# Fused attention, gated experts and a spatial gating MLP on one core: six warm-up products, batch 1's first adds on VectorE, the last batch's factors in three buffers with W2 behind them, w_out's last row off GpSimd

## The chip, the cores and the metric

The kernel runs on one core of one Trainium2 chip. The metric is the device time of one execution in microseconds (us). TensorE is called PE in the profile, VectorE DVE, ScalarE ACT, GpSimd POOL, SyncE SP. SyncE only issues transfers (DMA).

## The reference

Three layers follow one another on 4 batches of 448 positions. All of it is float32.

```python
scores = cap * np.tanh(scale * q @ k.T / cap)            # 12 heads of 64
x = softmax(scores) @ v                                  # then x: 4 x 448 x 768
# experts: 4 small causal attentions of width 64, two chosen for each position
ye = softmax(causal((x @ wq[e]) @ (x @ wk[e]).T / 8)) @ (x @ wv[e]) @ wo[e]
x = sum of the two chosen w[e] * ye
h = gelu(x @ w_in)                                       # 768 -> 1024
u, v = halves of h
gated = u * (w_sg @ layernorm(v) + b_sg)                 # w_sg mixes positions
out = x + gated @ w_out                                  # 512 -> 768
```

## The kernel before

Matmuls of the first layer run in float32; later ones split each operand into a rounded part and a remainder (names ending in h and l) and add three products. Since the experts' output enters the MLP through wo and w_in alone, the kernel multiplies these two first into W2 (tiles `parts`, `wt`, then `w2_d` in DRAM, read back as `w2_h` and `w2_l`).

**Attention** goes in slots, one for each pair of heads, six pairs for each of four batches (`slot`, L319). In a slot TensorE makes scores `s`, ScalarE applies Tanh and Exp into `p`, TensorE multiplies with the values into `po` and adds up the softmax sums from `pb`, a running sum of the `p` tiles. `scores` (L224) makes the first add of `pb` (L242): on VectorE in batch 0, on GpSimd in the others. `add_up` (L250) makes the other two on VectorE. At the very start, before anything has been loaded, `WARM` products of zeros keep TensorE busy (L771).

**Slots carry side work** at places named a, w, p and n. Through the first ten slots that is the conversion of w_in and its products into W2 (`prepare_weights`); then the experts of the batch before (`PLAN`), and the conversion of w_out, a row or half a row at a time (`w_out`, L423: VectorE unpacks two 32-bit halves, GpSimd rounds, subtracts and adds, SyncE stores both parts in DRAM as `wud`).

**Normalising** a batch: the sums go to DRAM (`rd`), come back spread over partitions as `ri` (`spread`), VectorE takes the reciprocal (`inverted`), they go to DRAM again, and come back copied over 64 partitions as factors `rb` (`load_rb`, L370, two transfers each). `over_sums` multiplies an output block `os` by its `rb`; `in_parts` splits it into `xh` and `xl`. A batch has three blocks. The factors' tiles are two (`rb0`, `rb1`), so the third block's loads take the first one's tile. `normed` (L389) says at which places of which slots this is done; for the last batch `slot` does it after the last pair (L349 to L355) and `experts_end` (L640) loads the third factors.

**The end** runs the experts of batches 2 and 3 and the MLP side by side (`experts_end`, `mlp_a`, `mlp_b`, `mlp_c`, ORD 3). `mlp_weights(0)` reads W2 through GpSimd's queue at high priority (L821 to L824); `mlp_weights(2)` converts w_out's last row in three pieces (L817). Temporary tiles `tmp` of the MLP and w_out's pieces share six buffers. In this part the order on each engine is chosen by the scheduler from the program and its own clock; before it, the engines keep the program's order, except SyncE, whose order is always the scheduler's.

Each engine works through its instructions in order; SyncE's queue likewise holds a transfer back until what it waits for is there, and all behind it.

Of the kernel before, what the change touches and what calls it, by code (L numbers as in the profile page):

```python
# [33 lines left out]
LO64, HI64 = (float(np.array([w], np.uint32).view(np.float32)[0]) for w in (0x38000000, 0x47F00000))  # L34
LAG, RATIO, LRATIO, AHEAD, EQ, ORD, L1, EL, WC, NCST, D0, D1, D2, PB, XE, SE, START, WARM, Q2, CK, PE, CP_, AD, WR, KD, PTA, PTE, XHA, LGA, SL, GL, YL, GA, GB = 0.4, .9, .35, 150, 1, 3, 1, 1, 500, 1, 3, 3, 2, 1, 1, 0, 500, 12, 1, 2, 0, 0, 0, 6, 0, 3, 2, 4, 4, 0, 0, 0, 1, 0
GC = float(np.float32(np.sqrt(2.0 / np.pi)))
# [38 lines left out]
def build(ctx: ExitStack, tc: tile.TileContext, a: dict):  # L75
    nc = tc.nc
# [147 lines left out]
    def scores(b, hp, h, qp, kp, then=None):  # L224
# [15 lines left out]
        if h == 0:  # L240
            pb = at.tile([128, 2, S], F32, tag="pb", name=f"pb{b}_{hp}", bufs=3)
            (dve if b == 0 else pool_e).tensor_tensor(pb, p[:, :, 0, :], p[:, :, 1, :], op=ALU.add)  # L242
            pend[b, hp] = (p, pb)
        else:
            p0, pb = pend[b, hp]
            pend[b, hp] = (p0, p, pb)
            if n == 2:
                ptail[b, hp // 2] = p[:, :, 1, :]
# [70 lines left out]
    def slot(i, side):  # L319
# [29 lines left out]
        if i == len(pairs):  # L349
            drain(sums(B - 1, HP // 2 - 1))  # L350
            invert(B - 1)
            spread(B - 1)
            inverted(B - 1)
            load_rb(B - 1, 0)
            load_rb(B - 1, 1)  # L355
        side("p")
# [12 lines left out]

    def load_rb(b, h2):  # L370
        rb = rbs[b, h2] = xp.tile([128, 2, S], F32, tag=f"rb{h2 % 2}", name=f"rb{b}_{h2}")
        for r in range(2):
            nc.sync.dma_start(rb[64 * r:64 * r + 64],
                              rb_d[b][r::2, h2:h2 + 1, :].rearrange("r o s -> o r s").to_broadcast([64, 2, S]))
# [14 lines left out]
    def normed(n, place):  # L389
# [14 lines left out]
        elif step == (3, "w"):  # L404
            over_sums(b, 0)
            over_sums(b, 1)
            load_rb(b, 2)
        elif b == 0 and step == (3, "a1"):
            in_parts(b, 0)
            in_parts(b, 1)  # L410
        elif step == (4, "w"):
            if b:
                in_parts(b, 0)
            over_sums(b, 2)
            if not b:
                in_parts(b, 2)
        elif b and step == (4, "a1"):
            in_parts(b, 1)
            in_parts(b, 2)

    projected = []

    def w_out(k, i, of, w, me):  # L423

# [6 lines left out]
        p, e = from64(w, me[:, :n], me[:, n:])  # L431
        rnd("p", hi, p)
        pool_e.tensor_tensor(p, p, hi.bitcast(F32), op=ALU.subtract)
        pool_e.tensor_tensor(lo, p, e, op=ALU.add)
        for t in range(2):
# [204 lines left out]
    def experts_end():  # L640
# [3 lines left out]
        def steps():  # L644
# [12 lines left out]
            over_sums(l, 1)  # L657
            load_rb(l, 2)
            yield from weigh(b, 1, 0, 1)
# [153 lines left out]
    def mlp_weights(part):  # L813
# [3 lines left out]
        if part == 2:  # L817
            for i in range(3):
                yield from w_out(3, i, 3, *[lambda dt, name: ml.tile([128, 512], dt, tag="tmp", name=name, bufs=6)] * 2)
            return  # L820
        for k in range(2):  # L821
            with tc.high_priority(12000):
                nc.gpsimd.dma_start(w2_h[:, k, :], w2_d[0][:, k, :])
                nc.gpsimd.dma_start(w2_l[:, k, :], w2_d[1][:, k, :])  # L824
        nc.sync.dma_start(gln, a["g_ln"])
# [140 lines left out]
    g_places = [(mg, "gh", "gl"), (mo, "pe2", "pe3"), (mo, "pt0", "pt1"), (mg, "gh", "gl")]  # L966
    MLP = 8 * 1278.0 + 8 * 1120.0 + 4 * 1120.0 + 36 * 560.0 + 17.0
    drain(mlp_weights(0))
    C = 36 * 560.0
# [77 lines left out]
```

## Time and profile before

| | us |
|---|---|
| runs, median (lowest to highest of 3) | 548.62 (545.62 to 549.73) |
| profiled execution | 545.04 |
| its span, first to last instruction | 543.2 |
| TensorE busy | 516.1 |
| VectorE busy | 333.2 |
| ScalarE busy | 319.0 |
| GpSimd busy | 132.2 |

The profile is of one execution. A timeline row gives start, length, engine, line, operation, what is written and read, and in brackets how long the engine had been idle before it and what ended that. The line is mostly that of a helper (L106 for three engines, L121 for matmuls), so tiles identify a row. A row "x4" joins four instructions that follow one another.

### The profile page before, as it was taken

How to read it: one execution, taken by the hardware profiler on the slowest of the kernel's cores; microseconds unless marked ns; L12 is line 12 of the kernel's file. 1: busy time of each engine (PE TensorE's matmuls, PEld its weight loads, DVE VectorE, ACT ScalarE, POOL GpSimd, SP SyncE). 2: the span in 40 equal slices, each digit the busy share in tenths (PEclk: the TensorE clock that was granted, in tenths of full speed). 3: DMA queues.
4: the chain of work that ended last, by engine and by line, in shares of the span. 5: the costliest groups of instructions: out<-in, count | busy, mean ns of one | idle time of the engine just before them, and what ended most of it. 6: DMA issues, size and time to landing. Idle time of an engine off the chain costs nothing.

```text
span 543.2 us, 7596 instructions
## 1 busy us (share of the span) xinstructions
PE 516.1 (95%) x2732; PEld 336.6 (62%) x2732; DVE 333.2 (61%) x683; ACT 319.0 (59%) x529; POOL 132.2 (24%) x151
## 2 busy tenths in 40 slices
PE   7999999899999999999998698999899999999997
PEld 2233333455655555554476457768678889889996
DVE  3899999874466646456724596755722796484300
ACT  5989888688777766777631573542544364252211
POOL 0000232251451341441540829004502010010000
PEclk9999999999999999999999899799999999999999
DMA  8955527643514224240129011110611000001011
GB/s 306 344 168 159 188 70 201 203 154 113 153 60 142 74 87 120 71 107 1 59 73 293 18 39 49 42 46 0 219 67 52 1 1 35 34 36 50 36 51 68
DMA packets 34693, 54.16 MB, mean 100 GB/s; under 512 B 5536, under 2 KB 29536, under 8 KB 34656
## 3 DMA queue, kind: packets, MB, share of 16 engines
q1 hardware_dynamic: 33360, 48.22, 28.6%
q0 software_dynamic: 1152, 5.24, 2.8%
q8 instruction: 21, 0.34, 0.3%
q10 hardware_dynamic: 144, 0.23, 0.1%
q14 instruction: 16, 0.13, 0.1%
HBM read 41.92 MB, written 11.75 MB: 99 GB/s over the span
## 4 chain that ended last, share of the span: by engine, by line
PE 71%; DVE 9%; ACT 5%; DMA 5%; POOL 4%; issue 4%; SPq 1%; DVEq 0%; POOLq 0%; ACTq 0%
PE o L121 15%; PE s L121 9%; PE po L121 9%; PE sp L121 7%; PE qk L121 5%; PE v L121 4%; PE hv L121 4%; PE hu L121 4%; PE w2ps L121 3%; PE a L121 3%; ACT p L106 3%; PE av L121 3%; DMA rb<-rd 3%; PE tr L542 2%; POOL pe L106 2%
## 5 line engine op out<-in xcount | busy, mean ns | idle before, releaser
L106 ACT ACTIVATE p<-s,tsc 128x896 f32<-128x896 f32 x84 | 80.7, 1005 | 26.0 <-PE s L121 20.2
L121 PE MATMUL s<-qp,kp 64*128 64x448 f32 (+1 forms) x384 | 77.8, 566 | 3.6 <-ACT p L106 3.6
L106 POOL TENSOR_TENSOR pb<-p 128x896 f32<-128x896 f32 x18 | 41.0, 2280 | 160.4 <-ACT p L106 153.6
L106 ACT ACTIVATE p<-p,capt 128x1792 f32<-128x1792 f32 (+1 forms) x48 | 77.0, 1604 | 1.1
L106 DVE TENSOR_TENSOR pb<-pb,p 128x896 f32<-128x896 f32 (+1 forms) x48 | 56.8, 1183 | 20.3 <-ACT p L106 11.1
L121 PE MATMUL po<-p,vv 128*64 128x448 f32 x288 | 59.4, 548 | 0.0
L121 PEld LDWEIGHTS s<-qp,kp 64*128 64x128 f32 (+1 forms) x384 | 27.0, 173 | 48.6 <-issue 23.4
L106 POOL TENSOR_SCALAR pe<-pe,cs 112x112 f32<-112x112 f32 (+1 forms) x64 | 39.7, 642 | 56.0 <-DVE cs L106 56.0
L106 ACT ACTIVATE pe<-a,m 112x112 f32<-112x112 f32 (+3 forms) x64 | 31.4, 495 | 26.7 <-DVE m L106 23.6
L106 DVE CUSTOM_DVE_ANT_0 a<-a,neg 112x112 f32<-112x112 f32 (+3 forms) x64 | 28.2, 463 | 29.8 <-PE a L121 29.3
L121 PEld LDWEIGHTS po<-p,vv 128*64 128x64 f32 x288 | 18.5, 136 | 37.9 <-issue 35.1
L121 PE MATMUL qk<-xh,wqk_h 128*128 128x448 f32 x96 | 37.3, 390 | 4.1 <-DVE xh L106 2.3
L106 POOL TENSOR_TENSOR rstd<-rstd,mhalf 112x1 f32<-112x1 f32 x16 | 10.2, 637 | 104.8 <-DVE rstd L106 104.8
L121 PE MATMUL o<-gh,wu_h 128*128 128x448 f32 x96 | 35.3, 368 | 0.0
L542 PE MATMUL tr<-ident,pe 112*112 112x112 f32 x160 | 25.3, 265 | 10.5 <-POOL pe L106 4.6
L106 ACT ACTIVATE ob<-o 128x448 f32<-128x448 f32 x24 | 13.0, 542 | 37.8 <-PE o L121 37.7
L121 PE MATMUL o<-gl,wu_h 128*128 128x448 f32 x96 | 35.2, 366 | 0.0
L121 PE MATMUL qk<-xh,wqk_l 128*128 128x448 f32 x96 | 35.1, 366 | 0.0
L121 PE MATMUL o<-gh,wu_l 128*128 128x448 f32 x96 | 34.8, 367 | 0.0
L106 ACT ACTIVATE pt<-tr 112x112 f32<-112x112 f32 (+3 forms) x48 | 18.8, 403 | 22.7 <-PE tr L542 22.3
L542 PEld LDWEIGHTS tr<-ident,pe 112*112 112x112 f32 x160 | 17.8, 134 | 18.6 <-issue 8.1
L121 PE MATMUL a<-qk 64*112 64x112 f32 (+3 forms) x128 | 28.6, 440 | 0.8 <-ACT qk L106 0.6
(227 smaller groups left out, 1113.2 us busy)
## 6 DMA issues: line engine op xcount, KB each, us to landing
rb<-rd SPq DMA_DIRECT2D x24, 224.0 KB, 5.4
out_dram<-ob SPq DMA_DIRECT2D x24, 224.0 KB, 1.9
kp<-in_kT_dram SPq DMA_DIRECT2D x23, 224.0 KB, 3.5
qp<-in_qT_dram SPq DMA_DIRECT2D x23, 224.0 KB, 3.7
vv<-in_v_dram SPq DMA_DIRECT2D x24, 192.0 KB, 3.3
wuw<-in_w_out_dram SPq DMA_DIRECT2D x6, 384.0 KB, 3.4
wud<-wuw SPq DMA_DIRECT2D x12, 192.0 KB, 1.9
ws<-in_wqk_dram SPq DMA_DIRECT2D x4, 384.0 KB, 5.7
```

Source lines behind the costliest of these rows:

```text
L106: ins = f(*args, **kw)
L121: pin(nc.tensor.matmul(*args, **kw))
L542: pin(nc.tensor.transpose(g[:CP, j * CP:(j + 1) * CP], pe[:, j * CP:(j + 1) * CP], ident))
```

## The change

Six edits in the text:

- `WARM` goes from 12 to 6.
- In `scores`, batch 1's pairs 0 to 3 make their first add of `pb` on VectorE.
- In `normed`, batch 0's third block is multiplied and split in slot 3's place p, not slot 4's place w.
- For the last batch, `spread`, `inverted` and the loads of factors move behind the attention, ahead of `mlp_weights(0)`, and the third factors get a tile of their own (in `ypool`, tag y), loaded with the other two.
- W2 is read through SyncE's queue, with no priority.
- `w_out` gets an argument `by`; for the last row ScalarE rounds, and VectorE subtracts and adds.

```diff
--- before.py
+++ after.py
@@ -32,7 +32,7 @@
 BIG = float(np.finfo(np.float32).max)
 
 LO64, HI64 = (float(np.array([w], np.uint32).view(np.float32)[0]) for w in (0x38000000, 0x47F00000))
-LAG, RATIO, LRATIO, AHEAD, EQ, ORD, L1, EL, WC, NCST, D0, D1, D2, PB, XE, SE, START, WARM, Q2, CK, PE, CP_, AD, WR, KD, PTA, PTE, XHA, LGA, SL, GL, YL, GA, GB = 0.4, .9, .35, 150, 1, 3, 1, 1, 500, 1, 3, 3, 2, 1, 1, 0, 500, 12, 1, 2, 0, 0, 0, 6, 0, 3, 2, 4, 4, 0, 0, 0, 1, 0
+LAG, RATIO, LRATIO, AHEAD, EQ, ORD, L1, EL, WC, NCST, D0, D1, D2, PB, XE, SE, START, WARM, Q2, CK, PE, CP_, AD, WR, KD, PTA, PTE, XHA, LGA, SL, GL, YL, GA, GB = 0.4, .9, .35, 150, 1, 3, 1, 1, 500, 1, 3, 3, 2, 1, 1, 0, 500, 6, 1, 2, 0, 0, 0, 6, 0, 3, 2, 4, 4, 0, 0, 0, 1, 0
 GC = float(np.float32(np.sqrt(2.0 / np.pi)))
 GQ = float(np.float32(np.sqrt(0.044715)))
 
@@ -239,7 +239,7 @@
         act.activation(p[:, :, :n, :], p[:, :, :n, :], AF.Exp, scale=capt)
         if h == 0:
             pb = at.tile([128, 2, S], F32, tag="pb", name=f"pb{b}_{hp}", bufs=3)
-            (dve if b == 0 else pool_e).tensor_tensor(pb, p[:, :, 0, :], p[:, :, 1, :], op=ALU.add)
+            (dve if b == 0 or (b, hp) < (1, 4) else pool_e).tensor_tensor(pb, p[:, :, 0, :], p[:, :, 1, :], op=ALU.add)
             pend[b, hp] = (p, pb)
         else:
             p0, pb = pend[b, hp]
@@ -349,10 +349,6 @@
         if i == len(pairs):
             drain(sums(B - 1, HP // 2 - 1))
             invert(B - 1)
-            spread(B - 1)
-            inverted(B - 1)
-            load_rb(B - 1, 0)
-            load_rb(B - 1, 1)
         side("p")
         if 0 < i < len(pairs):
             b, hp = pairs[i - 1]
@@ -367,8 +363,8 @@
 
     rbs = {}
 
-    def load_rb(b, h2):
-        rb = rbs[b, h2] = xp.tile([128, 2, S], F32, tag=f"rb{h2 % 2}", name=f"rb{b}_{h2}")
+    def load_rb(b, h2, pool=xp, tag=None):
+        rb = rbs[b, h2] = pool.tile([128, 2, S], F32, tag=tag or f"rb{h2 % 2}", name=f"rb{b}_{h2}")
         for r in range(2):
             nc.sync.dma_start(rb[64 * r:64 * r + 64],
                               rb_d[b][r::2, h2:h2 + 1, :].rearrange("r o s -> o r s").to_broadcast([64, 2, S]))
@@ -408,19 +404,19 @@
         elif b == 0 and step == (3, "a1"):
             in_parts(b, 0)
             in_parts(b, 1)
-        elif step == (4, "w"):
-            if b:
-                in_parts(b, 0)
+        elif b == 0 and step == (3, "p"):
             over_sums(b, 2)
-            if not b:
-                in_parts(b, 2)
+            in_parts(b, 2)
+        elif b and step == (4, "w"):
+            in_parts(b, 0)
+            over_sums(b, 2)
         elif b and step == (4, "a1"):
             in_parts(b, 1)
             in_parts(b, 2)
 
     projected = []
 
-    def w_out(k, i, of, w, me):
+    def w_out(k, i, of, w, me, by=None):
 
         n = DM // of
         o = slice(i * n, (i + 1) * n)
@@ -429,9 +425,10 @@
         nc.sync.dma_start(w.bitcast(I64), a["w_out"][:, k, o])
         yield WC
         p, e = from64(w, me[:, :n], me[:, n:])
-        rnd("p", hi, p)
-        pool_e.tensor_tensor(p, p, hi.bitcast(F32), op=ALU.subtract)
-        pool_e.tensor_tensor(lo, p, e, op=ALU.add)
+        rnd(by or "p", hi, p)
+        diff = dve if by else pool_e
+        diff.tensor_tensor(p, p, hi.bitcast(F32), op=ALU.subtract)
+        diff.tensor_tensor(lo, p, e, op=ALU.add)
         for t in range(2):
             nc.sync.dma_start(wu_d[t][:, k, o], (hi, lo)[t].bitcast(F32))
         yield 1.0
@@ -655,7 +652,6 @@
             yield from turn(b, 0, 0)
             over_sums(l, 0)
             over_sums(l, 1)
-            load_rb(l, 2)
             yield from weigh(b, 1, 0, 1)
             yield from turn(b, 0, 1)
             in_parts(l, 0)
@@ -816,12 +812,11 @@
             return
         if part == 2:
             for i in range(3):
-                yield from w_out(3, i, 3, *[lambda dt, name: ml.tile([128, 512], dt, tag="tmp", name=name, bufs=6)] * 2)
+                yield from w_out(3, i, 3, *[lambda dt, name: ml.tile([128, 512], dt, tag="tmp", name=name, bufs=6)] * 2, by="a")
             return
         for k in range(2):
-            with tc.high_priority(12000):
-                nc.gpsimd.dma_start(w2_h[:, k, :], w2_d[0][:, k, :])
-                nc.gpsimd.dma_start(w2_l[:, k, :], w2_d[1][:, k, :])
+            nc.sync.dma_start(w2_h[:, k, :].bitcast(F32), w2_d[0][:, k, :])
+            nc.sync.dma_start(w2_l[:, k, :].bitcast(F32), w2_d[1][:, k, :])
         nc.sync.dma_start(gln, a["g_ln"])
         nc.sync.dma_start(bsg, a["b_sg"].to_broadcast([128, S]))
         dve.memset(mhalf, -0.5)
@@ -965,6 +960,11 @@
     v_places = [(ml, "vh", "vl"), (xp, "xh", "xl")] * 2
     g_places = [(mg, "gh", "gl"), (mo, "pe2", "pe3"), (mo, "pt0", "pt1"), (mg, "gh", "gl")]
     MLP = 8 * 1278.0 + 8 * 1120.0 + 4 * 1120.0 + 36 * 560.0 + 17.0
+    spread(B - 1)
+    inverted(B - 1)
+    load_rb(B - 1, 0)
+    load_rb(B - 1, 1)
+    load_rb(B - 1, 2, ypool, "y")
     drain(mlp_weights(0))
     C = 36 * 560.0
     if ORD == 2:
```

SyncE's queue, from the last batch's sums on. `rs`, `rd`, `ri` and `rb` are the sums, their DRAM tile, their spread form and the factors; `wuw` is a half row of w_out and `wud` its store; the digit behind a name is batch or row. Before:

```order
L299 DMA rd3_2396<-rs3_2039 128x448
L308 DMA ri3_2398<-rd3_2396 32x42 x4
L314 DMA rd3_2396<-ri3_2398 32x42 x4
L373 DMA rb3_0_2408<-rd3_2396 64x2x448 x2
L373 DMA rb3_1_2411<-rd3_2396 64x2x448 x2
L436 DMA wud0_79<-wuw2_1_2333 128x384
L373 DMA rb3_2_2841<-rd3_2396 64x2x448 x2
L436 DMA wud1_80<-wuw2_1_2333 128x384
L830 DMA w_sgT0_2522<-in_w_sgT_dram 112x448
```

And in the change:

```order
L308 DMA ri3_2392<-rd3_2390 32x42 x4
L433 DMA wud0_79<-wuw2_1_2327 128x384
L314 DMA rd3_2390<-ri3_2392 32x42 x2
L433 DMA wud1_80<-wuw2_1_2327 128x384
L314 DMA rd3_2390<-ri3_2392 32x42 x2
L818 DMA w2_h_2488<-w2d0_81 128x1024
L369 DMA rb3_0_2503<-rd3_2390 64x2x448 x2
L369 DMA rb3_1_2506<-rd3_2390 64x2x448 x2
L369 DMA rb3_2_2509<-rd3_2390 64x2x448 x2
L819 DMA w2_l_2489<-w2d1_82 128x1024
L818 DMA w2_h_2488<-w2d0_81 128x1024
```

Two stores of w_out and the first quarter of W2 (`w2_h`) now stand ahead of the six factor transfers, which follow one another; the other three quarters stand behind them.

VectorE, at the products of the last batch's blocks (`os3`) with their factors; `a2_0_*_3` are expert scores of 448 columns of batch 2 that the instruction masks. Before:

```order
L106 RECIPROCAL ri3_2398<-ri3_2398 128x42
L106 TENSOR_SCALAR wum2_1_2334<-wuw2_1_2333 128x384
...
L106 SCALAR_TENSOR_TENSOR wum2_1_2334<-wuw2_1_2333,wum2_1_2334 128x384
L106 TENSOR_TENSOR os3_1_1971<-os3_1_1971,rb3_0_2408 128x896
L106 ISA a2_0_0_3_2625,m2_0_0_3_2629<-a2_0_0_3_2625,neg_74 112x448
...
L106 TENSOR_TENSOR os3_3_2180<-os3_3_2180,rb3_1_2411 128x896
L106 ISA a2_0_1_3_2626,m2_0_1_3_2633<-a2_0_1_3_2626,neg_74 112x448
...
L106 TENSOR_TENSOR os3_5_2369<-os3_5_2369,rb3_2_2841 128x896
...
L106 TENSOR_TENSOR gt2_2657<-vp2_2414 112x64
```

And in the change:

```order
L106 TENSOR_SCALAR wum2_1_2328<-wuw2_1_2327 128x384
...
L106 SCALAR_TENSOR_TENSOR wum2_1_2328<-wuw2_1_2327,wum2_1_2328 128x384
L106 RECIPROCAL ri3_2392<-ri3_2392 128x42
L106 ISA a2_0_0_2_2535,m2_0_0_2_2539<-a2_0_0_2_2535,neg_74 112x336
...
L106 ISA a2_0_0_3_2622,m2_0_0_3_2626<-a2_0_0_3_2622,neg_74 112x448
...
L106 ISA a2_0_1_3_2623,m2_0_1_3_2630<-a2_0_1_3_2623,neg_74 112x448
...
L106 TENSOR_TENSOR os3_1_1965<-os3_1_1965,rb3_0_2503 128x896
...
L106 TENSOR_TENSOR os3_3_2174<-os3_3_2174,rb3_1_2506 128x896
...
L106 TENSOR_TENSOR os3_5_2363<-os3_5_2363,rb3_2_2509 128x896
...
L106 TENSOR_TENSOR gt2_2654<-vp2_2393 112x64
```

w_out's unpacking now ends ahead of the reciprocal (`ri3`, which before stood ahead of it), and the two masks of 448 columns stand ahead of all three products.

TensorE, behind these expert scores (`v2_3` is a chunk of the experts' values, `hv0` and `hu0` are the MLP's first products with W2). Before:

```order
L121 MATMUL a2_0_0_3_2625<-qk2_0_2219 112x448
L121 MATMUL a2_0_1_3_2626<-qk2_0_2219 112x448
L121 MATMUL v2_3_2637<-wvg_h_77,xh2_2170 112x260
L121 MATMUL v2_3_2637<-wvg_l_78,xh2_2170 112x260
L121 MATMUL v2_3_2637<-wvg_h_77,xl2_2171 112x260
```

And in the change:

```order
L121 MATMUL a2_0_0_3_2622<-qk2_0_2213 112x448
L121 MATMUL a2_0_1_3_2623<-qk2_0_2213 112x448
L121 MATMUL hv0_0_2553<-w2_h_2488,yh0_2547 112x512
L121 MATMUL hv0_1_2614<-w2_h_2488,yh0_2547 112x512
L121 MATMUL hv0_2_2709<-w2_h_2488,yh0_2547 112x512
L121 MATMUL hv0_3_2750<-w2_h_2488,yh0_2547 112x512
L121 MATMUL hu0_0_2927<-yh0_2547,w2_h_2488 128x448
L121 MATMUL hu0_0_2927<-yl0_2548,w2_h_2488 128x448
L121 MATMUL v2_3_2634<-wvg_h_77,xh2_2164 112x260
L121 MATMUL v2_3_2634<-wvg_l_78,xh2_2164 112x260
```

Six products with W2 now stand ahead of the chunk of values. From about 373 us of the profile on, TensorE's order is that of before.

## Rows read from the trace of the kernel before

**Rows 1.** The page, part 1: busy us, share of the span, instructions of TensorE.
```profile
PE 516.1 (95%) x2732; PEld 336.6 (62%) x2732; DVE 333.2 (61%) x683; ACT 319.0 (59%) x529; POOL 132.2 (24%) x151
```

**Rows 2.** Busy time by stretch (us; x counts instructions), granted clock, DMA share, GB/s.
```profile
84.00:104.00 20.00, 17.58 (x80) 6.60 (x80) 19.70 (x20) 16.80 (x19) 5.51 (x2) 1.00 0.79 223
298.00:312.00 14.00, 9.44 (x41) 6.94 (x39) 8.52 (x22) 7.22 (x15) 10.60 (x11) 0.88 0.09 24
340.00:352.00 12.00, 11.22 (x43) 8.86 (x44) 8.71 (x22) 6.63 (x20) 0.76 (x2) 0.72 0.08 25
```

**Rows 3.** Timeline (start, us, engine line op out<-in, idle before), the start; one tile's durations; landings.
```profile
0.73 0.41 ACTq L106 DMA_DIRECT2D qp<-in_qT_dram  x1
1.32 5.30 PE L121 MATMUL warm<-z 128*128 128x512 bf16 x12 [1.32 <-POOL z L106]
6.54 2.01 PE L121 MATMUL s<-qp,kp 64*128 64x448 f32 x8
7.85 1.01 ACT L106 ACTIVATE p<-s,tsc 128x896 f32<-128x896 f32 x1 [5.18 <-PE s L121]
L121 PE MATMUL s<-qp,kp x72: 536/536/876, 6.5 to 38.6; 64*128 64x448 f32 x56, 64*64 64x448 f32 x16
qp<-in_qT_dram ACTq DMA_DIRECT2D x1, 224.0 KB, 3.0
```

**Rows 4.** Timeline of VectorE, GpSimd and TensorE, 78 to 105 us.
```profile
87.08 2.20 DVE L106 TENSOR_TENSOR pb<-pb,p 128x896 f32<-128x896 f32 x2
92.08 2.50 DVE L106 CAST xh<-os 128x896 fp32r<-128x896 f32 x1
95.63 0.62 DVE L106 CAST xh<-os 128x896 fp32r<-128x896 f32 x1
91.42 2.69 POOL L106 TENSOR_TENSOR pb<-p 128x896 f32<-128x896 f32 x1 [9.63 <-ACT p L106]
104.32 0.48 PE L121 MATMUL qk<-xh,wqk_h 128*128 128x448 f32 x1 [2.29 <-DVE xh L106]
```

**Rows 5.** Timeline of SyncE's queue, VectorE and TensorE, 279 to 305 us; median landings (DMA issues).
```profile
279.63 3.69 SPq L373 DMA_DIRECT2D rb<-rd  x4
286.41 1.28 SPq L373 DMA_DIRECT2D rb<-rd  x2
296.15 1.09 DVE L106 TENSOR_TENSOR os<-os,rb 128x896 f32<-128x896 f32 x1 [5.92 <-DMA rb<-rd]
282.68 1.01 PE L121 MATMUL a<-qk 64*112 64x448 f32 x4
287.79 0.47 PE L121 MATMUL qk<-xh,wqk_h 128*128 128x448 f32 x1 [1.76 <-ACT pe L106]
302.11 0.31 PE L542 MATMUL tr<-ident,pe 112*112 112x112 f32 x1 [2.93 <-POOL pe L106]
304.28 0.62 PE L542 MATMUL tr<-ident,pe 112*112 112x112 f32 x2 [1.63 <-POOL pe L106]
rb<-rd SPq DMA_DIRECT2D x24, 224.0 KB, 5.4
wi_4w<-in_w_in_dram SPq DMA_DIRECT2D x2, 512.0 KB, 3.7
w_l<-w2d POOLq DMA_DIRECT2D x2, 512.0 KB, 10.5
```

**Rows 6.** Timeline of GpSimd, ScalarE, VectorE and TensorE, 327 to 341 us; waits of SyncE's queue.
```profile
327.75 7.56 POOL L106 TENSOR_SCALAR pe<-pe,cs 112x112 f32<-112x112 f32 x8
338.19 0.54 ACT L106 ACTIVATE gsu<-hu 128x448 f32<-128x448 f32 x1 [3.50 <-POOL wuw L106]
338.77 0.62 DVE L106 SCALAR_TENSOR_TENSOR gsu<-gsu,hu 128x448 f32<-128x448 f32 x1 [4.51 <-ACT gsu L106]
340.78 0.47 PE L121 MATMUL hu<-yh,w_h 128*128 128x448 f32 x1 [2.61 <-DVE u L106]
SPq L436 <- POOL wuw L106: 63.2, 14, 21.3
```

## The prediction

> **What bounds the kernel now.** I read the busy times first. TensorE is busy 516.1 of 543.2 us [rows 1], so at most 27 us are to be had by taking its waits away, and no shorter engine matters except where TensorE waits for it. The busy times by stretch then show where it waits: 2.4 us in 84 to 104 us, where VectorE has no time left (19.70 of 20), 4.6 us in 298 to 312 us and 0.8 us in 340 to 352 us [rows 2]. In the last two the granted clock falls as well, to a mean of 0.88 and 0.72. There are two levels, 1.2 and 2.4 GHz, so a mean of c over t us stands for (1-c) x 2t at the lower level and costs (1-c) x t of full-speed work: 0.12 x 14 = 1.7 us and 0.28 x 12 = 3.4 us. Before each fall TensorE had stood idle for 2.93 [rows 5] and 2.61 us [rows 6]. Last I read the timeline around those places, to see whom TensorE waits for. The change touches all of them.
>
> **Part A, six warm-up products instead of twelve.** The twelve take 5.30 us, 0.44 each, from 1.32 us, and the first scores start at 6.54 [rows 3]. Their queries are sent for at 0.73 and land 3.0 later, at 3.7, so nothing but the products holds them. Six products end at 1.32 + 6 x 0.44 = 4.0, 2.6 earlier. Not all of it comes back. The first score matmuls take up to 876 ns, later ones 536, so up to about 7 us the lower level holds, although the stretch view prints 1.00 there (its clock record has not begun). Now the first scores lie in that time wholly. From their start to the first Tanh it is 7.85 - 6.54 = 1.31 now; at most 1.31 x 876/536 = 2.1 then, so Tanh starts at 6.1, 1.7 earlier. The second tile of scores takes 2.1 more, to 8.2, and its Tanh could have started at 7.85 + 1.01 = 8.9 before: 0.7 earlier. ScalarE's chain of Tanh and Exp sets the pace until 20 us, so I take 1.2, between the two; bounds 0 (clock later) and 2.6.
>
> By the Trainium skill, page "TensorE: Matmul & The Clock Gate", section "Part 1: The HAM clock gate (the "warmup" mystery)", activity releases the clock and the place where it rises is not tied to the kernel's start but varies from run to run. One profile cannot show the spread; it is a reason for the rival on the clock below.
>
> **Part B, batch 1's first adds of head pairs 0 to 3 on VectorE.** Four adds leave GpSimd (2.69 us for the one at 91.42) and cost VectorE what an add of the same size costs it, 2.20 / 2 = 1.10 each [rows 4], 4.4 together. But a GpSimd add is not free for VectorE: the cast that starts under the one at 91.42 takes 2.50 where the same cast alone takes 0.62, 1.88 more. The other three stretch a VectorE instruction in the same way. At 1.88 each VectorE gains 4 x (1.88 - 1.10) = 3.1 us before 104 us. What TensorE can take of that is its wait for the cast of the third normalised block, 2.29 at 104.32. The change also puts that block's product, cast and remainder ahead of the slot's running sum, but its factors' two loads behind four more transfers on SyncE's queue, and ScalarE waits for that sum, so some comes back as a wait of ScalarE. I take 1.8; bounds 0 (loads late) and 2.7 (the wait and some smaller ones).
>
> **Part C, last batch's factors in three buffers, W2 behind them.** Before, the third pair of factor loads waited until the first product had freed its buffer: the first four issue from 279.63, the third pair at 286.41, in the midst of W2's transfers, and VectorE stands 5.92 us at the third product until 296.15 [rows 5]. Behind it in VectorE's order stand the gates and the softmax factors, behind these GpSimd's scaling, and behind that the transposes for which TensorE waits 2.93 and 1.63. A wait of 1.76 at 287.79 comes from the same queue: the masks of 448 columns stood between the products; now they stand ahead of all three. Together 6.3 us of idle TensorE, and 1.7 us of lower clock.
>
> What is late next? On SyncE's queue two stores of w_out and W2's first quarter now stand ahead of the factors. The stores wait for GpSimd, whose input VectorE now prepares in its idle time before the reciprocal, so I cost them at their issue; with these and W2's quarter the factors start at about 281 instead of 279.63. Six issues at 3.69 / 4 = 0.92 end at 286.5, and with the median landing of 5.4 the last is there at 291 to 292, 4 to 5 us earlier than 296.15. From the third product to the transpose it took 302.11 - 296.15 = 6.0, now 297 to 298. TensorE came there at 302.11 - 2.93 = 299.2; less the 1.76, plus some 0.6 of W2 products moved ahead and 1.0 of a new wait, it comes at 299.0. So that wait goes, with 1.5 to spare.
>
> The new wait: six products with W2's first quarter now stand right behind the matmuls of 448 columns, which end at 282.68 + 1.01 = 283.7. The quarter (512 KB) is issued at about 280.2; a load of that size on this queue lands in 3.7 us, one of the same size from GpSimd's queue in 10.5. I take 4.5, near the first, because it is on the same queue and only two stores and small transfers stand ahead of it: 1.0 us of wait. Sum of C: 6.3 + 1.7 - 1.0 = 7.0; bounds -0.7 (landing 10.5 makes the wait 7.0, and the clock falls there instead: 6.3 - 7.0) and 8.0.
>
> **Part D, w_out's last row off GpSimd.** At 340.78 TensorE has waited 2.61 us: the up-projection's buffers are free only when GpSimd has done the row's pieces, and GpSimd starts on them after 7.56 us of scaling that begins at 327.75. ScalarE (3.50) and VectorE (4.51 until 338.77) stand idle for it [rows 6]. Now ScalarE rounds and VectorE subtracts and adds. Six operations of 256 columns cost VectorE at least 1.10 x 256/896 = 0.31 and at most what GpSimd's eight scalings take, 0.95 each: 1.9 to 5.7 us. I take 0.4 each, 2.4, near the smaller row since it is the same engine and kind; this fits in the 4.51 us in which it stood. ScalarE's three roundings fit in its 3.50. So the 2.61 goes and of the 3.4 us of lower clock I count 2.9, as other short waits are near: 5.5; bounds 1.4 (rival 3) and 6.0. W2's loads off GpSimd's queue cost nothing elsewhere, since GpSimd is idle there.
>
> By the Trainium skill, page "SBUF — State Buffer", section "Who interferes with whom", a VectorE instruction with two SBUF inputs and a GpSimd instruction that reads SBUF exclude each other, and the second to issue blocks in full. By that rule the six operations could each stand behind a scaling; the cast in rows 4 agrees that a VectorE instruction waits. This is the third rival below.
>
> **Sum.** 1.2 + 1.8 + 7.0 + 5.5 = 15.5 us. Against the profiled execution's own 545.04 us that is 529.5. The median of the runs, 548.62, lies 3.6 above it, and a timed median is asked for: 548.6 - 15.5 = 533.1.
>
> **Rivals.**
> (1) W2 is late, 0.11. If the quarter takes 10.5 us as from GpSimd's queue, it lands at 290.7: 7.0 us of wait instead of 1.0, and the clock falls there instead, 1.7. For it: TensorE is in order, and the loads of this stretch are the slowest of the kernel. Against it: the quarter is now first, not mixed with the factors. 533.1 + 6.0 + 1.7 = 540.8.
> (2) The clock rises later at the start, 0.06. If the lower level lasts 5.8 us longer (as long again as it did now), that costs up to 2.9 of full-speed work: part A turns from -1.2 to +1.7 and the time is 536.0. Against it: until 20 us ScalarE sets the pace.
> (3) VectorE is late at w_out, 0.05. At 5.7 us for the six it runs 5.7 - 4.5 = 1.2 over its idle time, TensorE still waits that long, and so the clock's 2.9 may stay lost: 533.1 + 4.1 = 537.2.
> (4) Slower than before, 0.05. SyncE's queue stands at a w_out store ahead of the factors' way back. For it: it has waited up to 21.3 us for GpSimd at such a store [rows 6], and everything on VectorE is queued behind the factors. The slack is the 1.5 us of part C. A stand of 21.3 would cost 19.8: 533.1 + 19.8 = 552.9. It decides against the change from a stand of 15.5 + 1.5 = 17.0 us on. Against it: the store's input is ready on VectorE some 2 us before the reciprocal.
> (5) Two or more parts miss their gain together, 0.11: with C and D at their lower bounds, 533.1 + 7.7 + 4.1 = 544.9.
>
> **Chances and range.** The forecast, all parts within their bounds with no rival, has 0.62. Within 1% (543.1 to 554.1) is about what a measurement of this kernel can't tell from no change. The forecast and rivals 1 to 3 lie below that: 0.84 faster. Rival 5 and part of rival 4 lie within: 0.13. Slower by over 1%: 0.03. The range reaches from 527.0 (all upper bounds at once, 19.3, give 529.3; the rest is for runs in which the clock falls less often) to 542.0, which takes in rivals 1 to 3 and leaves out 4 and 5, 0.16.
>
> **What would show it.** Warm-up ends near 4.0 and the first Tanh starts near 6. No GpSimd add before 95 us; the wait of 2.29 for the third block's cast gone. All six factor loads issued in one run from about 281; the third product starts by 292; no wait over 1 us at the transposes near 302 and the granted clock of that stretch 1.00. A wait of about 1 us for W2 near 283. No GpSimd operation on w_out after 320 and no wait over 1 us near 340, clock 1.00 there. Wrong would be: TensorE waiting for W2 for several us, the factors starting after 283, or VectorE's idle time at 335 gone while TensorE still waits for it.

## The result and the profile after

| | before | after |
|---|---|---|
| runs, median us (lowest to highest) | 548.60 (545.62 to 549.73, 4 runs) | 528.93 (527.34 to 531.75, 4 runs) |
| profiled execution | 545.04 | 528.26 |
| its span | 543.2 | 526.5 |
| TensorE busy | 516.1 | 509.7 |

The ratio is 0.9655, 95% interval 0.9598 to 0.9713: faster. One run of this document, of experiment e5, went at a granted clock of 0.56 throughout (837.38 us) and stands in no other figure. Busy times of the changed kernel (page, part 1), and the three stretches of [rows 2] with one more (us, busy time of PE, PEld, DVE, ACT and POOL, granted clock, DMA share, GB/s):

```profile
PE 509.7 (97%) x2726; PEld 333.6 (63%) x2726; DVE 331.0 (63%) x693; ACT 320.8 (61%) x532; POOL 111.7 (21%) x134
```

```profile
84.00:104.00 20.00, 19.81 (x92) 8.36 (x90) 16.83 (x19) 15.79 (x17) 2.09 (x1) 1.00 0.77 237
298.00:312.00 14.00, 13.17 (x72) 8.35 (x71) 11.40 (x34) 11.82 (x32) 5.97 (x6) 1.00 0.11 34
340.00:352.00 12.00, 12.00 (x81) 8.48 (x80) 5.99 (x17) 5.77 (x15) 0.55 (x1) 1.00 0.01 1
365.00:380.00 15.00, 13.15 (x67) 10.47 (x66) 8.74 (x27) 6.81 (x22) 4.71 (x8) 0.89 0.60 211
```

TensorE is busy 19.81 of 20 us in the first stretch (17.58 before), and the clock is 1.00 in the two where it had been 0.88 and 0.72. The last stretch is one in which the clock falls now: a lower clock, behind a wait of 1.85 us that stood in the kernel before as well (2.05 at 390.24) with the clock at 1.00 behind it. The timeline of the changed kernel (start, us, engine, line, operation, out<-in, idle before and its end) at the places of [rows 3 to 6]:

```profile
1.31 2.74 PE L121 MATMUL warm<-z 128*128 128x512 bf16 x6 [1.31 <-POOL z L106]
5.29 1.91 ACT L106 ACTIVATE p<-s,tsc 128x896 f32<-128x896 f32 x2 [2.62 <-PE s L121]
...
91.92 0.62 DVE L106 CAST xh<-os 128x896 fp32r<-128x896 f32 x1
...
272.42 0.42 DVE L106 RECIPROCAL ri<-ri 128x42 f32<-128x42 f32 x1 [1.68 <-DMA ri<-rd]
275.13 0.37 SPq L818 DMA_DIRECT2D w_h<-w2d  x1
275.79 4.67 SPq L369 DMA_DIRECT2D rb<-rd  x6
280.41 1.15 PE L121 MATMUL hv<-w_h,yh 128*112 128x512 f32 x4 [1.17 <-DMA w_h<-w2d]
286.78 1.09 DVE L106 TENSOR_TENSOR os<-os,rb 128x896 f32<-128x896 f32 x1 [1.08 <-DMA rb<-rd]
321.81 0.50 PE L539 MATMUL tr<-ident,pe 112*112 112x112 f32 x3 [0.88 <-POOL pe L106]
371.74 0.47 PE L539 MATMUL tr<-ident,pe 112*112 112x112 f32 x3 [1.85 <-ACT pe L106]
```

The first Tanh starts 2.6 us earlier. The cast that took 2.50 us beside GpSimd's add takes 0.62, and the wait of 2.29 near 104 us is gone. The six factor loads issue in one run behind W2's first quarter, the third product comes 14.4 us after the reciprocal (296.15 - 276.93 = 19.2 before, the first row of the fence on e6 below), the waits of 2.93, 1.63, 1.76 and 2.61 us are gone, and W2 is waited for 1.17 us. The same instructions of ScalarE in the two traces give the lead, the time by which the changed kernel is ahead, by place: 2.6 us up to 76 us, 4.5 from 109 to 282, 10.9 at 329, 17.6 at 364, 16.9 from 423 on.

### The profile page after: what moved, and what is told of

It reads as the page before. It is cut to its first block, busy times and chain, and to the rows that moved or that the text cites. A ratio compares the mean times of both kernels' runs of the same rounds, so it can differ in the third digit from the quotient of the medians.

```text
span 526.5 us, 7575 instructions
## 1 busy us (share of the span) xinstructions
PE 509.7 (97%) x2726; PEld 333.6 (63%) x2726; DVE 331.0 (63%) x693; ACT 320.8 (61%) x532; POOL 111.7 (21%) x134
## 4 chain that ended last, share of the span: by engine, by line
PE 70%; DVE 13%; ACT 6%; DMA 4%; issue 3%; POOL 3%; SPq 1%; DVEq 0%; POOLq 0%; ACTq 0%
PE o L121 16%; PE po L121 8%; PE s L121 8%; PE qk L121 7%; PE sp L121 7%; PE v L121 5%; PE hv L121 4%; ACT p L106 4%; PE a L121 3%; PE hu L121 3%; PE av L121 3%; PE tr L539 3%; DVE pb L106 3%; DMA rb<-rd 2%; POOL pe L106 1%
## 5 line engine op out<-in xcount | busy, mean ns | idle before, releaser
L106 DVE TENSOR_TENSOR pb<-pb,p 128x896 f32<-128x896 f32 (+1 forms) x48 | 53.2, 1109 | 19.7 <-ACT p L106 10.5
L106 POOL TENSOR_TENSOR pb<-p 128x896 f32<-128x896 f32 x14 | 29.9, 2134 | 167.1 <-PE po L121 93.5
L106 POOL TENSOR_SCALAR pe<-pe,cs 112x112 f32<-112x112 f32 (+1 forms) x64 | 37.8, 615 | 57.6 <-DVE cs L106 57.6
L106 ACT ACTIVATE pt<-tr 112x112 f32<-112x112 f32 (+3 forms) x48 | 18.8, 404 | 17.2 <-PE tr L539 16.9
L121 PE MATMUL v<-wvg_h,xh 128*112 128x260 f32 x96 | 28.5, 296 | 0.1
```

The source lines that it names most:

```text
L106: ins = f(*args, **kw)
L121: pin(nc.tensor.matmul(*args, **kw))
```

## The experiments

Each kernel was run on a chip beside the kernel before. "Lost" is (1 - granted clock) x span, the full-speed time that the lower level takes, as a mean over the runs. Over 115 runs a straight line per kernel with one slope fits: each us lost costs 0.78 us (standard error 0.06). "At 1.00" is that line's time at a granted clock of 1.00 (standard errors 0.4 to 0.5; below, "error" is that of a difference). The four runs of the kernel before in the first table are not among the 115: their clocks are not on record. On the three chips of the experiments the kernel before stands at 540.6, 540.4 and 539.7 by this line, so less than about 1 us between kernels of different chips says nothing. The ratios of the changed kernel and of its variants (e8, e10 to e12) have different medians of the kernel before under them, 548.60 against 546.54 and 545.88, and are compared with that in mind. Code is shown in part (`...`), against the kernel before, for e8 and e10 to e12 against the changed kernel.

| kernel | median us (runs) | ratio (95%) | lost | at 1.00 |
|---|---|---|---|---|
| before (three chips) | 546.91, 546.54, 545.88 (39) | | 8.1 | 540.2 |
| changed | 528.93 (4) | 0.9655 (0.9598 to 0.9713) | 1.9 | 527.8 |
| e1 six warm-up products | 544.17 (7) | 0.9950 (0.9928 to 0.9971) | 6.8 | 539.0 |
| e2 adds, third block | 543.04 (6) | 0.9926 (0.9902 to 0.9950) | 6.2 | 538.3 |
| e3 factors and W2 | 539.99 (6) | 0.9856 (0.9826 to 0.9886) | 5.6 | 535.3 |
| e4 w_out | 541.07 (6) | 0.9893 (0.9868 to 0.9917) | 5.5 | 537.0 |
| e5 factors only (last two columns with e9's one run, 540.20) | 542.12 (6) | 0.9903 (0.9868 to 0.9938) | 6.6 | 536.3 |
| e6 W2 only | 540.16 (6) | 0.9867 (0.9838 to 0.9895) | 4.4 | 536.1 |
| e7 adds only | 544.00 (10) | 0.9943 (0.9921 to 0.9965) | 6.4 | 538.7 |
| e8 changed, wo off GpSimd | 527.97 (6) | 0.9651 (0.9622 to 0.9680) | 2.0 | 526.2 |
| e10 changed, no warm-up | 531.69 (6) | 0.9750 (0.9721 to 0.9779) | 1.1 | 531.1 |
| e11 changed, six adds, wo | 526.69 (6) | 0.9645 (0.9614 to 0.9676) | 1.4 | 525.4 |
| e12 changed, two buffers | 529.53 (6) | 0.9714 (0.9686 to 0.9743) | 1.8 | 528.6 |

### Each part alone (e1 to e4)

```diff
-... START, WARM, ... = ... 500, 12, ...
+... START, WARM, ... = ... 500, 6, ...
```

> The kernel before with WARM 6 alone. Theory: the granted clock rises about 0.5 us after the first scores whatever came ahead of them, so all of the 2.6 us by which the warm-up is shorter is kept: first Tanh at about 5.3 us instead of 7.85, like-numbered instructions of ScalarE 2.6 us earlier up to the end, ratio 0.995. Rival (the prediction's own term): the clock rises at about 7 us as before, the first scores lie at the lower level, first Tanh near 6.1 and later ones 1.2 earlier, ratio 0.998. Second rival: the gain is kept until about 80 us and then lost in the stretch where VectorE has no time left: nothing left at 110 us, ratio 1.000.

The ratio is the theory's 0.995, but not for its reason: of the 2.7 us between the medians 1.2 are left at 1.00, the rest is less lost clock. In the trace the first Tanh starts at 5.94 (7.85 before), later ones are 1.5 to 1.8 us earlier up to 280 us: between theory and rival. What scatters is the start itself. With twelve products, in seven traces in which nothing ahead of 60 us differs, the first Tanh starts between 7.02 and 7.85, with six in five traces between 5.29 and 5.94; at the third Tanh the means are 10.93 and 9.37. So part A is worth 1.6 us, not the 2.6 that the first pair of profiles shows: that pair holds the latest of one kind and the earliest of the other. The second rival is out: of 1.75 us at 76 us 1.55 are still there at 110 us.

```diff
-            (dve if b == 0 else pool_e).tensor_tensor(pb, ...)
+            (dve if b == 0 or (b, hp) < (1, 4) else pool_e).tensor_tensor(pb, ...)
...
+        elif b == 0 and step == (3, "p"):
             over_sums(b, 2)
+            in_parts(b, 2)
...
```

> The kernel before with batch 1's first adds of pairs 0 to 3 on VectorE and the third block of batch 0 normalised in slot 3, and nothing else. Theory: the adds on GpSimd stretch VectorE's instructions by some 1.9 us each, so VectorE gains although it does more; TensorE's wait of 2.29 us near 104 us is gone and like-numbered instructions are 1.9 us earlier from 110 us on, ratio 0.9965. Rival: the part gains only with the shorter warm-up ahead of it (other phase of ScalarE against VectorE): under 0.5 us at 110 us, ratio 1.000.

The wait near 104 us is gone, and of the lead 0.8 us belongs to the start, 1.8 to part B, kept from 109 to 282 us. The theory holds for the waits and the lead. Its ratio of 0.9965 lies outside the interval: at 1.00 the gain is 1.9 us, and 1.9 us less of the clock is lost.

```diff
...
+    load_rb(B - 1, 2, ypool, "y")
...
-                nc.gpsimd.dma_start(w2_h[:, k, :], w2_d[0][:, k, :])
+            nc.sync.dma_start(w2_h[:, k, :].bitcast(F32), w2_d[0][:, k, :])
```

> The kernel before with the last batch's factors in three buffers and W2 behind them on SyncE's queue, and nothing else. Theory: the third product starts 4.5 us earlier than 296.15, the waits of 2.93 and 1.63 us near 302 to 304 us go, the granted clock of 298 to 312 us is 1.00, one new wait of about 1.2 us for W2 near 283 us; like-numbered instructions 6.4 us earlier at 329 us of the kernel before, the clock still falls near 341 us as it did, ratio 0.988. Rival: TensorE, now earlier, only waits longer at w_out's last row on GpSimd near 340 us, and at most half is left behind it: 3 us, ratio 0.994.

The lead grows by 6.3 us between 282 and 329 us, the transposes are no longer waited for, and the clock of 298 to 312 us is 1.00. A new wait of 1.44 us stands at W2's first products near 286 us. The wait near 340 us stays (2.61), it does not grow. The theory holds.

```diff
...
-        rnd("p", hi, p)
-        pool_e.tensor_tensor(p, p, hi.bitcast(F32), op=ALU.subtract)
...
+        rnd(by or "p", hi, p)
+        diff = dve if by else pool_e
+        diff.tensor_tensor(p, p, hi.bitcast(F32), op=ALU.subtract)
...
```

> The kernel before with w_out's last row rounded on ScalarE and its remainders on VectorE, and nothing else. Theory: the wait of 2.61 us near 340 us goes and the granted clock of 340 to 352 us is 1.00; like-numbered instructions 6 to 6.7 us earlier at 364 us, ratio 0.988; the waits and the lower clock near 302 us stay. Rival (the prediction's lower bound): VectorE's six operations stand behind GpSimd's scalings, TensorE still waits 1.2 us there and the clock falls all the same: 1.4 us, ratio 0.997. Second rival: what is won here is given back at the wait for ScalarE's tile pe near 390 us: 4 us left in the span, ratio 0.993.

The lead grows by 6.3 us between 329 and 364 us, the wait near 340 us is gone, the clock of 340 to 352 us is 1.00. The first rival is out. So is the second: the lead is 4.2 us at 364 us and 4.1 from 423 us on, so nothing is given back near 390 us; it is no more than 4 because 2.3 us were lost between 282 and 329 us, where the clock stayed low for longer in this execution (0.76 in 298 to 312 us, 0.88 before). In the changed kernel the six operations on VectorE take 0.42, 0.42, 0.81, 0.41, 0.42 and 0.42 us. At 1.00 the four parts alone take 1.2, 1.9, 4.9 and 3.2 us off, 11.2 together, the changed kernel 12.4: the gap is within the errors, so no dependence of the parts on one another is shown.

### What carries part C (e5, e6, e9, e12)

```diff
...
+    spread(B - 1)
+    inverted(B - 1)
+    load_rb(B - 1, 0)
+    load_rb(B - 1, 1)
+    load_rb(B - 1, 2, ypool, "y")
...
```

> The kernel before with the last batch's factors in three buffers and moved behind the attention; W2 still through GpSimd's queue at high priority. Theory (the third buffer carries part C): the six loads issue in one run from about 280 us, the third product starts at 292.5 as with both halves (296.15 before), the waits of 2.93 and 1.63 us near 302 to 304 us go, ratio 0.987. Rival (W2's place carries it): W2's 2 MB run beside the six loads, which land 2 us or more later than with both halves, the third product starts at 294.5 or later, about half is left, ratio 0.993 or more.

e9 below is the same kernel, run once more for its trace.

```diff
-            with tc.high_priority(12000):
-                nc.gpsimd.dma_start(w2_h[:, k, :], w2_d[0][:, k, :])
+            nc.sync.dma_start(w2_h[:, k, :].bitcast(F32), w2_d[0][:, k, :])
```

> The kernel before with W2 read through SyncE's queue without priority; factors with two buffers at their old place. Theory (the buffer carries part C): the third pair of loads still waits for the first product, the third product starts within 1 us of 296.15, ratio 1.000 within 0.003. Rival: with W2 out of the way the first four loads land 3 us earlier, all three products follow, third product at 293, ratio 0.992. Second rival, on the other side: W2 is now late for the products of the MLP that stand ahead of the values' chunk, TensorE waits several us for it near 290 us, ratio 1.008.

> The kernel of e5 once more, for its trace at full clock (that of e5 was taken at a granted clock of 0.56 and says nothing of transfers). Theory after e6 (W2's transfers beside them are what makes the factors late; a third buffer only lets the last two issue earlier): the six loads issue in one run from about 280 us, but the last ones land 7 us or more after their issue, third product at 294 us or later of a span aligned with the kernel before, against 292.5 in e3 and e6. Rival (the third buffer is enough by itself): third product at 292.5, as in e3 and e6.

Timelines of VectorE, GpSimd's and SyncE's queue, and TensorE: first the kernel before (more in [rows 5]), then e6, then e9.

```profile
276.93 0.42 DVE L106 RECIPROCAL ri<-ri 128x42 f32<-128x42 f32 x1 [4.97 <-DMA ri<-rd]
283.38 1.29 POOL L823 DMA_DIRECT2D w_h<-w2d  x2
284.65 1.08 POOL L824 DMA_DIRECT2D w_l<-w2d  x2
```

```profile
277.86 0.42 DVE L106 RECIPROCAL ri<-ri 128x42 f32<-128x42 f32 x1 [4.95 <-DMA ri<-rd]
280.56 3.33 SPq L373 DMA_DIRECT2D rb<-rd  x4
287.42 1.23 SPq L373 DMA_DIRECT2D rb<-rd  x2
289.38 0.38 SPq L822 DMA_DIRECT2D w_h<-w2d  x1
292.55 1.09 DVE L106 TENSOR_TENSOR os<-os,rb 128x896 f32<-128x896 f32 x1 [2.41 <-DMA rb<-rd]
```

```profile
277.65 0.42 DVE L106 RECIPROCAL ri<-ri 128x42 f32<-128x42 f32 x1 [1.82 <-DMA ri<-rd]
278.63 1.30 POOL L818 DMA_DIRECT2D w_h<-w2d  x2
279.90 1.12 POOL L819 DMA_DIRECT2D w_l<-w2d  x2
284.55 5.72 SPq L369 DMA_DIRECT2D rb<-rd  x6
293.64 1.09 DVE L106 TENSOR_TENSOR os<-os,rb 128x896 f32<-128x896 f32 x1 [7.62 <-DMA rb<-rd]
298.29 1.08 DVE L106 TENSOR_TENSOR os<-os,rb 128x896 f32<-128x896 f32 x1
300.19 0.31 PE L538 MATMUL tr<-ident,pe 112*112 112x112 f32 x1 [1.23 <-POOL pe L106]
```

In e6 the third pair of loads still issues 6.9 us behind the first, as before (6.8), and yet it lands in 3.7 and 4.5 us. Before, in the midst of W2's quarters, it took 7.7 and 9.1. So the third product comes 14.7 us after the reciprocal instead of 19.2, as early as with both halves (292.54 - 277.85 = 14.7 in e3). In e9 no load waits for a buffer, but W2's four quarters go out ahead of the loads. Of the four small stores `rd` in front of the loads the last two land in 5.2 and 6.9 us instead of 1.4, and the loads land in 7.6 (median) instead of 5.2. The first product comes 16.0 us after the reciprocal (8.4 before), the third 20.6 us (19.2 before); the third stands for 0.9 of these behind VectorE's own work, its last load had landed at 297.40. So it was W2's two megabytes in flight, not the buffer, that made the factors late; my theory of e5 and e6 falls, that of e9 holds. What no run separates is W2's queue from its time of issue: e6 changes both. e9 gains all the same, by the order that comes with the edit: the masks stand ahead of the products, the wait of 1.76 us is gone, and of 2.93 and 1.63 at the transposes 1.23 and 0.93 are left. In e6 the scheduler, for which W2 comes later, puts other work ahead on TensorE, and the wait of 2.61 us near 340 us goes too; so e6's whole gain does not measure the transfers alone. At 1.00 the factors alone take 3.9 us off, W2 alone 4.1, both 4.9: the medians do not tell the halves apart, the traces do.

```diff
...
-    def load_rb(b, h2, pool=xp, tag=None):
+    def load_rb(b, h2):
...
+            load_rb(l, 2)
...
-    load_rb(B - 1, 2, ypool, "y")
...
```

> The changed kernel with the last batch's factors in two buffers at their old place, W2 on SyncE's queue. Theory (W2 off the factors' way is enough, the third buffer adds nothing): the third product starts within 0.5 us of 286.8 us as in the changed kernel though it still waits for the first product's buffer, no wait over 1 us at the transposes near 297 us, ratio to the kernel before within 0.003 of 0.9655. Rival (the third buffer is needed once the other parts are made): the third product at 289 us or later, transposes waited for again, ratio 0.972 or more.

The third product comes at 287.78, 14.9 us after the reciprocal (14.4 in the changed kernel). A wait of 1.69 us for ScalarE's `pe` at 283.70 stands where the changed kernel has 1.17 for W2, and the order behind it differs; after its later start of 0.5 us is taken off, it is 1.0 us behind at 355 us and 1.6 from 440 us on. Its ratio lies between what theory and rival gave, and its interval overlaps the changed kernel's. The medians are 529.53 against 528.93, at 1.00 it is 0.8 us above (error 0.6): the third buffer and the order that comes with it are worth about one of part C's us, and these runs do not tell that from nothing or from two.

### The adds, the start, and what is left (e7, e10, e8, e11)

```diff
-            (dve if b == 0 else pool_e).tensor_tensor(pb, ...)
+            (dve if b == 0 or (b, hp) < (1, 4) else pool_e).tensor_tensor(pb, ...)
```

> The kernel before with batch 1's first adds of pairs 0 to 3 on VectorE; the third block of batch 0 stays in slot 4. Theory (the adds carry part B, the moved block only follows): instructions 2.5 us earlier up to 95 us, TensorE's wait of 2.29 us near 104 us shrinks below 1 us, 1.5 to 2 us kept at 110 us, ratio 0.994 to 0.997. Rival (the moved block takes the wait away): the block's cast still stands behind the two running sums of slot 4, the wait of about 2 us near 104 us stays, less than 0.7 us kept at 110 us, ratio 0.999.

TensorE still waits 1.85 us for the block's cast, as the rival says, but 2.0 - 0.8 = 1.2 us is kept at 110 us, which it does not. So, in these two traces, the adds carry 1.2 of part B and the moved block 0.6.

```diff
-... START, WARM, ... = ... 500, 6, ...
+... START, WARM, ... = ... 500, 0, ...
```

> The changed kernel without any warm-up product. Theory (the clock rises some 3 to 6 us after the first product of any kind, as in the runs so far, 1.3 us to 4.5 to 7.1 us): scores start when the queries are there, at 3.8 us, the clock rises between 7 and 9.5 us, the first scores run at the lower level, Tanh of the third tile (second pair) is 0.5 to 2 us later than with six, ratio to the kernel before 0.968 to 0.970. Rival (the rise follows the first scores by 0.5 us, as both first profiles read): first Tanh at 5.2 us or earlier, ratio 0.965 or less.

Timelines of TensorE and ScalarE without warm-up (e10):

```profile
4.07 5.84 PE L121 MATMUL s<-qp,kp 64*128 64x448 f32 x20 [4.07 <-DMA kp<-in_k_cap_dram]
5.97 1.01 ACT L106 ACTIVATE p<-s,tsc 128x896 f32<-128x896 f32 x1 [3.31 <-PE s L121]
```

The clock record begins, at the upper level, at 9.06 us here, against 4.49 to 6.40 with six products (five traces) and 5.29 to 7.06 with twelve (seven). With twelve products it rises ahead of the first scores in five of the seven traces (in e7 at 5.29, scores from 5.95), so it does not follow them; without any it comes 5.0 us after the first product. The rival is out. In this trace the first Tanh starts at 5.97, the third at 10.20, 0.8 us behind the mean with six; by 28 us 2.0 us behind the changed kernel's trace. In this trace W2 is waited for 2.62 us as well, 1.4 more than in the changed kernel's. The ratio of 0.975 is more of a loss than the 0.968 to 0.970 that I had worked out, in part because the kernel before ran faster beside it (545.88). The medians lie 2.8 us apart, at 1.00 it is 3.3 (error 0.6).

```diff
-... GA, GB = ... 1, 0
+... GA, GB = ... 1, 11
```

> The changed kernel with the conversion of wo (last constant 11 for 0) rounded on ScalarE and its remainder on VectorE, off GpSimd. Theory: the wait of 1.85 us for the tile pe near 372 us comes from GpSimd, which has wo's 6 us ahead of pe and slows VectorE's gates beside it; the wait goes below 0.5 us, the granted clock of 365 to 380 us is 1.00, span 1.5 to 3 us shorter than the changed kernel's, ratio to the kernel before 0.961. Rival: VectorE and ScalarE are what is late there; 4 to 6 us more work on them makes the gates later, the wait stays or grows, ratio 0.966 to 0.970.

GpSimd in the changed kernel, and the stretch in e8:

```profile
355.30 2.03 POOL L106 TENSOR_SCALAR wo_h<-wo 128x384 fp32r<-128x384 f32 x4 [10.93 <-PE v L121]
357.30 3.97 POOL L106 TENSOR_TENSOR wo_l<-wo,wo_h 128x384 fp32r<-128x384 f32 x4
361.48 4.29 POOL L106 TENSOR_SCALAR pe<-pe,cs 112x112 f32<-112x112 f32 x8 [0.20 <-DVE cs L106]
```

```profile
365.00:380.00 15.00, 15.00 (x84) 13.29 (x83) 8.27 (x29) 6.42 (x18) 7.67 (x14) 1.00 0.60 211
```

The wait near 372 us is gone and TensorE is busy 15.00 of 15 us at full clock. But in this execution W2's first quarter was late: 2.61 us of wait near 282 us and a clock of 0.86 in 278 to 290 us, 2.8 us together, so the span shows nothing of it. The theory holds for the wait, while its ratio of 0.961 lies outside the interval. At 1.00 it is 1.6 us below the changed kernel (error 0.6); the ratios can't be told apart.

```diff
-            (dve if b == 0 or (b, hp) < (1, 4) else pool_e).tensor_tensor(pb, ...)
+            (dve if b == 0 or (b, hp) < (1, 6) else pool_e).tensor_tensor(pb, ...)
...
-... GA, GB = ... 1, 0
+... GA, GB = ... 1, 11
```

> The changed kernel with all six first adds of batch 1 on VectorE, and with wo's conversion on ScalarE and VectorE as in e8. Theory: in the changed kernel TensorE waits for nothing between 102 and 155 us, so the two further adds bring nothing there (like-numbered instructions within 0.3 us of the changed kernel at 140 us); the wait of 1.85 us near 372 us goes as in e8 and is worth 1.5 us; ratio to the kernel before 0.962 to 0.965. Rival: each add off GpSimd is worth another 0.5 us to TensorE as the first four were: 1.0 us earlier at 140 us, ratio 0.960 to 0.963. Second rival: VectorE, now with both adds, is late for a product near 115 us: later by 0.5 us or more at 140 us.

The theory was that TensorE waits for nothing there; it falls. By 102 us this trace gains 1.0 us on the changed kernel's (from 0.6 behind at the start to 0.4 ahead), as much as the rival says, but not add by add: all of it comes at the first of the two adds, and behind the second, at 108 us in the changed kernel, the lead stays at 0.4. The waits that go are mostly hidden in the busy time of TensorE: eight products of the sums take 1.36 us instead of 1.96. VectorE's product `os` that starts beside GpSimd's add in the changed kernel takes 2.33 us, here 1.09. e11 has the lowest median, but its ratio is not separated from the changed kernel's by these runs; by the fit, which has no term for the chip, it is 2.4 us below (error 0.6).

### Which wait costs the clock

One profile before showed two falls, behind the waits near 302 and 340 us. The same waits, untouched, in other traces (granted clock of the stretch around or behind the wait):

| wait of TensorE | clock 1.00 behind it | lower behind it |
|---|---|---|
| 2.3 us near 104 us | before, e1, e4 | e3, e6, e9 (0.83 in 102 to 112 us each) |
| 2.6 to 3.3 and 1.3 to 1.6 us near 302 us | none | before (0.88 in 298 to 312 us), e1, e2, e4, e7 (0.76 each) |
| 2.6 us near 340 us | e2, e7, e9 | before, e1 (0.72 in 340 to 352 us), e3 (0.72 in 335 to 347 us) |
| 2.05 us near 384 to 390 us | before, e1, e4 | e2, e3, e6, e7, e9 (0.83 over 10 us) |

For instance the same wait before (first fence) and in e2:

```profile
390.24 0.47 PE L542 MATMUL tr<-ident,pe 112*112 112x112 f32 x3 [2.05 <-ACT pe L106]
388.00:398.00 10.00, 7.95 (x45) 6.56 (x44) 4.78 (x18) 5.32 (x18) 0.55 (x1) 1.00 0.69 265
```

```profile
387.41 0.53 PE L542 MATMUL tr<-ident,pe 112*112 112x112 f32 x3 [2.06 <-ACT pe L106]
385.00:395.00 10.00, 7.94 (x36) 6.47 (x36) 4.95 (x18) 5.34 (x18) 0.55 (x1) 0.83 0.70 270
```

Behind the pair of waits near 302 us the clock falls in all five traces, and it stays up there where the pair is gone (e3, e6, the changed kernel and its variants); in e9, with 1.23 and 0.93 us left of it, it falls (0.88). The single waits of 2.05 to 2.6 us are followed by a fall in some executions and not in others, so such a fall belongs to none of them in particular. The kernels with fewer such waits lost less clock in the mean of their runs: 8.1 us before, 1.1 to 2.0 in the changed kernel and its variants; but e1, with the same waits as before, lost 6.8. The executions are not independent at each place: before, e1 and e4, with no fall near 104 and 390 us, are the three of these eight traces in which the clock rose latest at the start (6.40 to 7.06 us; 5.29 to 5.67 in the others). What ties the two together these runs leave open.

## Why the prediction was right, and where it was not

The time of 528.93 lies in the range (527.0 to 542.0) and "faster" was likeliest; 533.1 was 4 too high. Against the profiled execution, for which the sum was made, 529.5 stands beside 528.26. By the fit, the change took 12.4 us of work and waits and 0.78 x 6.2 = 4.8 us of clock, 17.2 together. The sum had 10.9 and 4.6, or 15.5. The rest of the 4 us lies in the four runs of the kernel before: their median of 548.60 is 2.1 above that of its 39 later runs (546.47). At 1.00, without the clock, the parts stand so: A 1.2 said and 1.2 measured, B 1.8 and 1.9, C 5.3 and 4.9, D 2.6 and 3.2.

- **A**, said 1.2, measured 1.6 on the mean of the traces (2.6 in the profiled pair, 1.2 at 1.00). The step that made the term small does not hold: that the lower level holds to about 7 us whatever is ahead. With six products the clock rose at 4.49 to 6.40. Six happens to be enough: at zero the loss that rival 2 describes comes.
- **B**, said 1.8, measured 1.8 (e2) and 1.9. The reason, GpSimd's adds stretching VectorE's instructions, bears out (2.33 against 1.09 in e11). That the running sum of the slot would then be the next thing late shows too: in e11 the products of that sum wait less, and 1.0 us more is gained.
- **C**, said 7.0, measured 6.4 in the lead of the changed kernel from 282 to 329 us. Third product by 291 to 292: it came 4.8 us sooner after the reciprocal, which is 291.3. That was luck in its terms: the last load issued about 2 us earlier than the sum had it (279.26, or 283.8 with the lead of 4.5, for 285.6) and took 2 us longer to land (7.4 for 5.4). Wait for W2 1.0: 1.17, in three later executions 2.61 to 2.78, a part of rival 1. In the other traces in which the pair of waits stands the clock costs 3.4 us there, not 1.7. And the mechanism was half wrong. I wrote that the third pair of loads waited for the first product's buffer, and this carried the 5.92 us. It does wait so; what made it late is what I mentioned beside it, that it issued in the midst of W2's transfers. e6 and e9 show it: with the wait for the buffer kept and W2 behind, the pair lands in 3.7 and 4.5 us instead of 7.7 and 9.1. The number came out because the change does both.
- **D**, said 5.5, measured 6.3 to 6.7 in the traces, of which 3.4 is the clock, which may or may not fall there: 3.2 us on the mean at 1.00. VectorE's six operations took 2.9 us for 2.4 said; rival 3 would have needed more than 4.5.
- **Rival 4** did not occur: the two stores ahead of the factors issued at 271.43 and 273.68, and held nothing back.
- **The clock.** I bound 1.7 and 3.4 us to two waits and counted 4.6; the mean of the runs has 4.8. The first binding held, the second did not: near 340 us the clock falls in three of six traces, and the waits near 104 and 390 us, to which I gave no clock, lose it in three of six and five of eight. That the total fits is partly luck.

## What to carry to other kernels

Where a transfer lands late, look at what else is in flight before blaming the wait that issued it late: moving two megabytes behind the small loads did what the extra buffer was built for. An edit that changes a scheduler's order gains or loses by the order too, so test its halves apart and read their traces: here each half alone took 3.9 to 4.1 us off and both together 4.9. Where the clock falls after short waits, count what all runs lose, not where one profile lost it.

## What was unexpected

- Untouched code starts differently from run to run: the first Tanh of the kernels with twelve warm-up products spreads over 0.83 us.
- A run's granted clock explains much of the spread between the runs of one kernel: its standard deviation is 1.5 us, and 0.9 around the fit.
- A TensorE that shows busy almost throughout can still wait: e11 gains 1.0 us between 94 and 104 us, where the changed kernel showed busy 9.81 of 10 us.
